# A float32 attention, expert and relu² kernel: the float64 weights converted earlier by way of DRAM, and half of the last network in seven block products

## The chip, the core and the metric

The kernel runs on one core of a Trainium2 chip. The core has a matrix engine (TensorE, PE in the profile), a vector engine (VectorE, DVE), a scalar engine (ScalarE, ACT), a general engine (GpSimd, POOL) and an engine whose queue issues most transfers (SyncE, SP); every queue works its instructions in order. The time is the device time of one launch in microseconds. Three runs of the kernel before took 679.74 to 681.3 us, median 680.23.

## The reference

Three parts follow on each other, all in float32 unless said otherwise: an attention with a window of 128, four dense experts whose sum is weighted per token, and a network with a squared relu.

```python
x = attention(q, k, v)                     # 2 x 8 heads, 576 positions, 64 wide -> 1152 x 512
p = domain_probs / (domain_probs.sum(-1, keepdims=True) + 1e-09)
for e in range(4):                         # w1: 512 x 1024, w2: 1024 x 512 each
    out += p[:, e:e + 1] * (np.maximum(x @ w1[e], 0.0) @ w2[e])
h = np.maximum(out @ w_in, 0.0)            # w_in: 512 x 2048, float64
y = (h * h @ w_out).astype(np.float32)     # w_out: 2048 x 512, float64
```

w_in and w_out arrive as float64 (their float32 draws are multiplied by a float64 scale); the kernel sees them as pairs of 32-bit integers.

## The kernel before

A float32 product is made of three matmuls on a rounded type (fp32r): with a = ah + al and b = bh + bl, the products ah·bh, al·bh and ah·bl are summed in PSUM. So each weight tile has a high part (wh, or ha and hs) and a low part (wl, la, ls), each activation too (xh, xl; hmem for the hidden layer). The last network is cut in two of the experts' size, so that there are six networks e = 0 to 5 with F = 1024: e = 4 and 5 are the first and the second half of w_in and w_out.

Tokens lie along the columns of the first GEMM and along the rows of the second. The first GEMM comes in items. A single item (`gemm1`) makes 128 hidden features for a chunk of 384 tokens with 12 matmuls. A pair item (`gemm1_pair`) makes 256 hidden features for all of 512 or 640 tokens as a 2 x 2 block product in seven block products for eight, each of 6 matmuls of 256 or 320 columns: 42 matmuls. It needs forms of the weights (sums of blocks, `w_forms`) and of the tokens (`x_forms`). Its epilogue reads the block products out of PSUM as p1 and p5 (copies by ScalarE, lines 989 and 994), adds them (VectorE, 975), applies relu (ScalarE, 979) and takes the low part (VectorE, 980). Three PSUM banks are reused inside an item: p1 must have been copied before the fourth block product writes that bank on, u2 before the fifth.

Expert 0 and the first half of expert 1 run in single items, the rest of the experts in 20 pair items, and both halves of the last network, e = 4 and 5, in 24 single items each. The second GEMM (`gemm2`, `gemm2_pair`, 512 columns a matmul) of an item is put off: items wait in the list `pend` and are flushed one or more items later (`flush_one`), so that the epilogue has time. e = 5 has 288 matmuls in its first GEMM and 216 in its second; its epilogue is relu on ScalarE (1037), the square on VectorE (1038), rounding on ScalarE (1039), low part on GpSimd (1040).

Up to the end of the first items a planner orders the work by costs and due times. From there the order is written by hand: the loop over `items` issues the matmuls, and after every few of them `fill(share, us)` moves a program clock on by `us` and takes some closures from a list of background work, the weights' preparation above all, whose number is set by `pace` so that a weight is ready some 14 us before its item. `loads` issues the next weight's transfer on SP when enough of the 24 weight buffers (4 KB per partition each) are free. Each weight item of e < 4 is one transfer of 512 KB, rounded to its high part by ScalarE and, for the low part, subtracted by GpSimd in pieces of 128x256.

A weight of e = 4 or 5 comes in two raw halves of 512 KB (128x512 float64 each) and goes through `split64` in its own buffers (wroom), just before its use: ScalarE scales the magnitude of the upper words (199), VectorE takes the sign (203), clamps (206), joins the low bits (210) and shifts and joins (214), all as integers; then ScalarE rounds the half to wh (349) and VectorE takes wl (429). This happens from about 418 us on.

Of the kernel before, what the change touches and what calls it, by code (L numbers as in the profile page):

```python
# [8 lines left out]
F32 = mybir.dt.float32  # L9
# [121 lines left out]
def kernel(  # L131
# [29 lines left out]
    ctx.enter_context(tc.manual_schedule())  # L161
    const = ctx.enter_context(tc.tile_pool(name="const", bufs=1))
# [21 lines left out]
    def split64(raw, n, t):  # L184

        lo, hi = raw[:, :, 0], raw[:, :, 1]  # L190
        stt = nc.vector.scalar_tensor_tensor

        def begin():
            if not room:
                room.extend(w_tile([P, 2, n], F32, "wroom")[0] for _ in range(3))
            room.append(room.pop(0))
            t["a"], t["b"] = room[-1][:, 0, :], room[-1][:, 1, :].bitcast(I32)
            t["ai"] = t["a"].bitcast(I32)
            nc.scalar.activation(out=t["a"], in_=hi.bitcast(F32), func=ACTF.Abs, scale=65536.0)

        return [
            begin,
            lambda: nc.vector.tensor_scalar(
                out=t["b"], in0=hi, scalar1=-(1 << 31), scalar2=None, op0=ALU.bitwise_and
            ),
            lambda: nc.vector.tensor_scalar(
                out=t["a"], in0=t["a"], scalar1=8053063680.0, scalar2=2.0,
                op0=ALU.min, op1=ALU.max,
            ),
            lambda: stt(  # L210
                out=t["b"], in0=lo, scalar=29, in1=t["b"],
                op0=ALU.logical_shift_right, op1=ALU.bitwise_or,
            ),
            lambda: stt(
                out=t["ai"], in0=t["ai"], scalar=3, in1=t["b"],
                op0=ALU.logical_shift_left, op1=ALU.bitwise_or,
            ),
        ]

# [10 lines left out]
    room = []  # L230
    raws = {}
    ready = set()
    carry = []
# [12 lines left out]
    def w_load(i):  # L246
        e, g, k = order[i]
        src, nk, nf = w_src(e, g, k)
        raws[i] = []
        if e < E:  # L250
            raw = w_tile([P, nk * nf], F32, "wraw")
            nc.sync.dma_start(out=raw[0].rearrange("p (k f) -> p k f", k=nk), in_=src)
            raws[i].append(raw)
        else:
            n = nk // 2
            for h in range(2):
                raw = w_tile([P, n * nf, 2], I32, "wraw64")
                nc.sync.dma_start(
                    out=raw[0].rearrange("p (k f) t -> p k (f t)", k=n).bitcast(mybir.dt.int64),
                    in_=src[:, h * n:(h + 1) * n, :],  # L260
                )
                raws[i].append(raw)


# [10 lines left out]
    def w_forms(i):  # L275
# [7 lines left out]
        def begin():  # L283
            for name, n in (("ha", 6), ("hs", 8), ("la", 6), ("ls", 8)):
                t[name] = w_tile([P, n, P], F32R, name)
            w1t[e, g] = [t[x] for x in ("ha", "hs", "la", "ls")]
# [25 lines left out]
        def done():  # L312
            for o in range(0, 8, 2):
# [14 lines left out]
            lambda: (part_lo(4, 2, a22), free.append(buf)),  # L328
# [4 lines left out]
    def w_ops(i):  # L333
# [3 lines left out]
        n = nk if e < E else nk // 2  # L337
        parts = (w1t, w2t)[k]
# [3 lines left out]
        def begin():  # L342
            parts[e, g] = [w_tile([P, nk, nf], F32R, name) for name in ("wh", "wl")]

        def part(full, h):
            (hi, _), (lo, _) = parts[e, g]
            ks = slice(h * n, (h + 1) * n)
            full = full.rearrange("p (k f) -> p k f", k=n)
            nc.scalar.activation(out=hi[:, ks, :], in_=full, func=ACTF.Copy)  # L349
            if e >= E:  # L350
# [1295 lines left out]
```

## Time and profile before

| | |
|---|---|
| median of three runs | 680.23 us |
| profiled execution | 680.41 us, its span 678.4 us |
| granted TensorE clock, mean over the span | 0.995 |
| busy, share of the span: PE, DVE, ACT, POOL | 98%, 60%, 44%, 42% |
| moved by DMA | 47.60 MB |

The profile shows one execution. Its span goes from the first to the last instruction that the trace holds; the time of the execution has 2.0 us more around it. The slices of the page show the stages: TensorE's digit is 8 in the first slice (17 us), 7 in the last and 9 in all between, and the granted clock is at full speed from the second slice on. The pair items lie between 227 and 457 us, the start of the last network's first half (e = 4) at about 475, its second half (e = 5) at about 575 to 674. A busy TensorE is not TensorE at its peak: to see what a matmul costs in a stream without holes, the distance from one start to the next is read, since the durations of neighbours overlap.

### The profile page before, as it was taken

What the parts mean: (1) busy time and instruction counts of PE and PEld (TensorE: products, weight loads), DVE (VectorE), ACT (ScalarE), POOL (GpSimd) and SP (SyncE); (2) the same over time, 40 slices, a digit from 0 to 9 for tenths busy, and PEclk for the clock granted to TensorE, in tenths of its full rate; (3) what the DMA queues carried; (4) which work ended last, traced back from release to release, by engine and by line L of the source; (5) the groups of instructions that cost most, each with busy time, mean ns of one, the idle gap of its engine ahead of it and who ended that gap; (6) DMA issues with size and microseconds to landing.
All of it is one profiled execution on the core that took longest, in us unless ns stands there. A gap on an engine that the chain in (4) does not pass through costs nothing.

```text
span 678.4 us, 10321 instructions
## 1 busy us (share of the span) xinstructions
PE 667.0 (98%) x3792; PEld 595.5 (88%) x3792; DVE 404.9 (60%) x905; ACT 297.2 (44%) x697; POOL 283.8 (42%) x359
## 2 busy tenths in 40 slices
PE   8999999999999999999999999999999999999997
PEld 7777888889999998888989899898899999999996
DVE  4798898854665346435553654887777788721212
ACT  5798787632331423133333324333555544422222
POOL 3799996518770455143464533000222222222222
PEclk7999999999999999999999999999999999999999
DMA  7933222021300112101201111136114200010101
GB/s 208 284 100 96 71 77 62 11 94 62 125 32 0 32 32 94 39 28 59 63 31 63 63 63 63 62 125 240 70 63 157 92 1 1 1 44 3 46 1 46
DMA packets 37106, 47.60 MB, mean 70 GB/s; under 512 B 3392, under 2 KB 25408, under 8 KB 37056
## 3 DMA queue, kind: packets, MB, share of 16 engines
q1 hardware_dynamic: 37056, 46.95, 22.1%
q8 instruction: 29, 0.48, 0.3%
q14 instruction: 21, 0.17, 0.1%
HBM read 44.58 MB, written 2.36 MB: 69 GB/s over the span
## 4 chain that ended last, share of the span: by engine, by line
PE 89%; POOL 4%; ACT 3%; DVE 2%; issue 1%; SPq 1%; DMA 1%; POOLq 0%; ACTq 0%
PE hps L865 24%; PE yacc L1051 23%; PE yacc L1019 18%; PE hps L965 15%; PE xps L660 3%; PE tp L788 2%; POOL wl L429 2%; PE sc L740 2%; POOL ts L776 1%; PE hps L1460 1%; SPq L1284 1%; DMA pt<-in_probs_dram 1%; POOL vl L429 1%; PE xtp L1084 0%; DVE st L768 0%
## 5 line engine op out<-in xcount | busy, mean ns | idle before, releaser
L1051 PE MATMUL yacc<-wh,hmem 128*128 128x512 f32 x488 | 157.1, 391 | 0.0
L1040 POOL TENSOR_TENSOR hmem<-r,hmem 128x384 fp32r<-128x384 f32 x48 | 50.0, 1042 | 200.7 <-ACT hmem L1039 198.9
L865 PE MATMUL hps<-xh,wh 128*128 128x384 f32 (+1 forms) x352 | 115.3, 328 | 1.0 <-DVE xl L1089 1.0
L1019 PE MATMUL yacc<-wh,hmem 128*128 128x512 f32 x360 | 115.3, 391 | 0.0
L865 PE MATMUL hps<-xh,wl 128*128 128x384 f32 (+1 forms) x352 | 113.8, 323 | 0.0
L865 PE MATMUL hps<-xl,wh 128*128 128x384 f32 (+1 forms) x352 | 113.6, 323 | 0.0
L1051 PEld LDWEIGHTS yacc<-wh,hmem 128*128 128x128 f32 x488 | 91.6, 188 | 18.6
L1051 PE MATMUL yacc<-wl,hmem 128*128 128x512 f32 x244 | 95.4, 391 | 0.0
L1019 PEld LDWEIGHTS yacc<-wh,hmem 128*128 128x128 f32 x360 | 67.6, 188 | 13.5
L429 POOL TENSOR_TENSOR wl<-wraw,wh 128x256 fp32r<-128x256 f32 (+1 forms) x70 | 61.9, 912 | 24.6 <-ACT wh L349 19.1
L1019 PE MATMUL yacc<-wl,hmem 128*128 128x512 f32 x180 | 70.3, 390 | 0.0
L865 PEld LDWEIGHTS hps<-xh,wh 128*128 128x128 f32 x352 | 66.3, 188 | 2.4 <-DVE xl L1089 1.2
L865 PEld LDWEIGHTS hps<-xl,wh 128*128 128x128 f32 x352 | 66.3, 188 | 0.9 <-issue 0.2
L865 PEld LDWEIGHTS hps<-xh,wl 128*128 128x128 f32 x352 | 66.3, 188 | 0.0
L1038 DVE TENSOR_TENSOR r<-hps,r 128x384 f32<-128x384 f32 x48 | 26.7, 556 | 64.2 <-ACT r L1037 64.2
L429 POOL TENSOR_TENSOR ls<-wsum,hs 128x256 fp32r<-128x256 f32 x40 | 32.3, 838 | 77.2 <-ACT hs L310 77.2
L1051 PEld LDWEIGHTS yacc<-wl,hmem 128*128 128x128 f32 x244 | 45.8, 188 | 8.6
L1037 ACT ACTIVATE r<-hps 128x384 f32<-128x384 f32 x48 | 23.4, 488 | 65.0 <-PE hps L865 65.0
L776 POOL TENSOR_SCALAR ts<-ts,st 128x256 f32<-128x256 f32 (+2 forms) x80 | 40.5, 521 | 25.7 <-DVE st L771 11.5
L979 ACT ACTIVATE hmem<-c 128x256 fp32r<-128x256 f32 (+1 forms) x60 | 25.8, 445 | 53.2 <-DVE c L975 52.4
L975 DVE TENSOR_TENSOR u<-hps,p 128x256 f32<-128x256 f32 (+1 forms) x40 | 18.2, 456 | 51.6 <-PE hps L965 50.2
L1069 DVE SCALAR_TENSOR_TENSOR y<-yacc,pt,y 128x512 f32<-128x512 f32 x54 | 38.9, 746 | 14.5 <-PE yacc L1019 8.2
(140 smaller groups left out, 1399.9 us busy)
## 6 DMA issues: line engine op xcount, KB each, us to landing
wraw<-in_w_dram SPq DMA_DIRECT2D x32, 512.0 KB, 3.6
wraw<-in_w_in_dram SPq DMA_DIRECT2D x16, 512.0 KB, 4.7
wraw<-in_w_out_dram SPq DMA_DIRECT2D x16, 512.0 KB, 3.4
rq<-in_qT_dram SPq DMA_DIRECT2D x8, 256.0 KB, 7.2
out_dram<-y SPq DMA_DIRECT2D x8, 256.0 KB, 2.1
rk<-in_kT_dram SPq DMA_DIRECT2D x8, 192.0 KB, 6.0
rv<-in_v_dram SPq DMA_DIRECT2D x8, 192.0 KB, 4.0
rq<-in_qT_dram SPq DMA_DIRECT2D x8, 192.0 KB, 2.6
```

The lines of the kernel that those rows point to most:

```text
L429: e.tensor_tensor(out=out, in0=in0, in1=f32(in1), op=ALU.subtract)
L660: nc.tensor.matmul(out=xps[:, :, o0:o0 + w], lhsT=l_, rhs=r_, start=(i == 0 and l_ is wh_ and r_ is hi), stop=(i == len(mm) - 1 and l_ is ...
L776: nc.gpsimd.tensor_scalar(out=ts[0:n, g, :], in0=ts[0:n, g, :], scalar1=st[0:n, 2, g:g + 1], scalar2=1.0, op0=ALU.mult, op1=ALU.mult,)
L865: nc.tensor.matmul(out=ps, lhsT=l_[:, k, cs], rhs=r_[:, k, cols], start=(k == 0 and r_ is xh and l_ is wh and not second), stop=(k == KT - ...
L965: nc.tensor.matmul(out=ps, lhsT=a[l_][:, k, :], rhs=b[r_][:, k, :], start=start and k == 0 and l_ == r_, stop=stop and k == 1 and l_ == 1, ...
L979: nc.scalar.activation(out=hh, in_=src, func=ACTF.Relu)
L1019: nc.tensor.matmul(out=y, lhsT=l_[:, ns], rhs=r_[:, fo, :], start=(first and fo == 0 and j == 0), stop=(last and fo == FTQ - 1 and j == 2),)
L1037: nc.scalar.activation(out=r, in_=ps, func=ACTF.Relu)
L1038: nc.vector.tensor_tensor(out=r, in0=ps, in1=r, op=ALU.mult)
L1040: nc.gpsimd.tensor_tensor(out=hl, in0=r, in1=f32(hh), op=ALU.subtract)
L1051: nc.tensor.matmul(out=y, lhsT=l_[:, ns], rhs=r_[:, fo, :], start=(first and j == 0), stop=(last and j == 2),)
L1069: nc.vector.scalar_tensor_tensor(out=yt, in0=y, scalar=pt[:, nt, e:e + 1], in1=yt, op0=ALU.mult, op1=ALU.add)
```

## The change

It has two parts.

The first: all 32 raw halves of w_in and w_out are converted during the experts. `convert` takes three weight buffers (two for raw halves, one for two results) as soon as three kept ones are free, which is during the first half of expert 1. Per half it issues one ScalarE and four VectorE instructions (266 to 277: magnitude, clamp, shift left by 3, join of the sign, join of the low bits); ScalarE's queue then stores the float32 half to DRAM (line 251, 256 KB) and loads the next raw half but one (239, 512 KB). These closures run at no more than 0.6 per us, at a single item's end, in a flush, or at the end of a pair item (`calm`). When a network weight's turn comes, `w_load` takes it from DRAM as float32 on SP in one transfer of 512 KB, and it is prepared like any expert's: ScalarE rounds, GpSimd subtracts in four pieces. `split64` and its buffers are gone.

The second: e = 5 runs in 8 pair items (4 weight groups x 2 token chunks), so its first GEMM has 336 matmuls, 168 of 256 and 168 of 320 columns; the second GEMM is the same. The epilogue of these items has the square (989 to 1009). The token forms for them are made by VectorE during e = 4. The weight forms (`w_forms`) take one buffer less.

On ScalarE at the end of the last 256-column item of expert 1: first the rows of before, where c_2884 to c_2886 are sums of an item's block products, p_2986 and p_2987 the next item's first copies.

```order
L979 ACTIVATE hmem<-c_2884 128x256 [waits DVE_49]
L979 ACTIVATE hmem<-c_2885 128x256 [waits DVE_49]
L979 ACTIVATE hmem<-c_2886 128x256 [waits DVE_49]
L989 ACTIVATE p_2986<-hps 128x320 [waits PE_49,Activation_49]
L994 ACTIVATE p_2987<-hps 128x320 [waits PE_49,Activation_49]
```

Now the same place, with p_3045 the next item's first copy; the numbers in brackets name what a row waits for, DMAHW a transfer.

```order
L1008 ACTIVATE hmem<-c_2937 128x256 [waits DVE_49]
L1008 ACTIVATE hmem<-c_2938 128x256 [waits DVE_49]
L266 ACTIVATE wconv<-wraw_2433 128x512 [waits DMAHW2_49,DMAHW1_49]
L251 DMA w_3007<-wconv 128x512
L239 DMA wraw_2432<-in_w_in_dram 128x2x256 [waits Activation_49]
L266 ACTIVATE wconv<-wraw_2432 128x512 [waits DMAHW6_49,DMAHW5_49]
L251 DMA w_3007<-wconv 128x512 [waits DVE_49]
L239 DMA wraw_2433<-in_w_in_dram 128x2x256 [waits DMAHW0_49,Activation_49]
L1018 ACTIVATE p_3045<-hps 128x320 [waits PE_49]
```

Between the last relu and p stand two halves, each with a store and a raw load; the second half reads wraw_2432, which the row above it loads.

At the end of the next 320-column pair of items in expert 1 the rows after the last relu are, in words: a half, store, load, the rounding of the weight sums hs, a half that reads what was just loaded, store, load, the rounding of a w2 weight, and then the next item's p. Before there were hs, p and the rounding behind p's.

On ScalarE at the start of e = 4: r and hmem are the epilogue of a single item, xh rounds a tile of transposed tokens for the same network, wh a weight. Before:

```order
L1037 ACTIVATE r<-hps 128x384 [waits PE_49]
L1039 ACTIVATE hmem<-r 128x384 [waits DVE_49]
L349 ACTIVATE wh<-wroom 128x512
L1088 ACTIVATE xh<-xtp 128x4x128 [waits PE_49]
L1037 ACTIVATE r<-hps 128x384 [waits PE_49]
L1039 ACTIVATE hmem<-r 128x384 [waits DVE_49]
```

And now:

```order
L1066 ACTIVATE r<-hps 128x384 [waits PE_49,Activation_49]
L1068 ACTIVATE hmem<-r 128x384 [waits DVE_49]
L266 ACTIVATE wconv<-wraw_2433 128x512 [waits DMAHW7_49,DMAHW0_49]
L251 DMA w_5321<-wconv 128x512
L239 DMA wraw_2432<-in_w_in_dram 128x2x256 [waits Activation_49]
L1118 ACTIVATE xh<-xtp 128x4x128 [waits PE_49]
```

The rounding of a weight half is gone, and a half, its store and a raw load stand ahead of xh. Some items later two halves in a row (half, store, load, a half that reads what was just loaded, store, load) come ahead of the copies of the second GEMM's results and the next xh, where two weight halves and their roundings stood among those copies.

On TensorE in e = 5: the end of a flush (yacc) and the start of the next item (hps), before:

```order
L1051 MATMUL yacc<-wh,hmem 128x512 x2
L1051 MATMUL yacc<-wl,hmem 128x512
L1051 MATMUL yacc<-wh,hmem 128x512
L865 MATMUL hps<-xh,wh 128x384 [waits DVE_49]
L865 MATMUL hps<-xl,wh 128x384
L865 MATMUL hps<-xh,wl 128x384
```

And now, where ht_5845 is a form of the tokens:

```order
L1048 MATMUL yacc<-wl,hmem 128x512
L1048 MATMUL yacc<-wh,hmem 128x512
L978 MATMUL hps<-xh,ha 128x320
L978 MATMUL hps<-xl,ha 128x320
L978 MATMUL hps<-xh,la 128x320
L978 MATMUL hps<-xh,ha 128x320
L978 MATMUL hps<-xl,ha 128x320
L978 MATMUL hps<-xh,la 128x320
L978 MATMUL hps<-ht_5845,hs 128x320 [waits DVE_49]
```

Instead of 12 matmuls of 384 columns on the plain weights there are groups of six of 320 (or 256) on weight forms.

The diff, cut to what the text speaks of:

```diff
     def w_load(i):
         e, g, k = order[i]
         src, nk, nf = w_src(e, g, k)
-        raws[i] = []
+        raw = w_tile([P, nk * nf], F32, "wraw")
         if e < E:
-            raw = w_tile([P, nk * nf], F32, "wraw")
             nc.sync.dma_start(out=raw[0].rearrange("p (k f) -> p k f", k=nk), in_=src)
-            raws[i].append(raw)
         else:
...
+            nc.sync.dma_start(out=raw[0], in_=single[i])
+        raws[i] = [raw]
+    single = {}
+    stored = set()
+    keep = [3]
...
+    def convert():
+        n = KT * FQ // 2
+        todo = [(i, h) for i in range(len(order)) if order[i][0] >= E for h in range(2)]
+        places = [w_tile([P, n, 2], I32, "wraw64") for _ in range(2)]
+        both, buf = w_tile([P, 2, n], F32, "wconv")
+        raw, ops = {}, []
+        at = {}
+        def load(j, eng):
+            i, h = todo[j]
+            src, nk, nf = w_src(*order[i])
+            raw[j] = places[j % 2][0]
+            m = nk // 2
+            eng.dma_start(
+                out=raw[j].rearrange("p (k f) t -> p k (f t)", k=m).bitcast(mybir.dt.int64),
+                in_=src[:, h * m:(h + 1) * m, :],
+            )
+            at["raw", j] = clock["now"] + 6.0
+        def swap(j):
+            i, h = todo[j]
+            if not by(at["out", j]):
+                return False
+            if h == 0:
+                single[i] = scratch.tile([P, 2 * n], F32, name=f"w{i}")
+            nc.scalar.dma_start(out=single[i][:, h * n:(h + 1) * n], in_=both[:, j % 2, :])
+            at["gone", j] = clock["now"] + 5.0
+            if h:
+                stored.add(i)
+            if j + 2 < len(todo):
+                load(j + 2, nc.scalar)
+        def steps(j):
+            a = both[:, j % 2, :]
+            ai = a.bitcast(I32)
+            def begin():
+                if not (by(at["raw", j]) and by(at.get(("gone", j - 2), 0.0))):
+                    return False
+                hi = raw[j][:, :, 1]
+                nc.scalar.activation(out=a, in_=hi.bitcast(F32), func=ACTF.Abs, scale=65536.0)
+            def shift():
+                nc.vector.tensor_scalar(
+                    out=a, in0=a, scalar1=8053063680.0, scalar2=2.0, op0=ALU.min, op1=ALU.max
+                )
+                nc.vector.tensor_scalar(
+                    out=ai, in0=ai, scalar1=3, scalar2=None, op0=ALU.logical_shift_left
+                )
+            def join(part, amount, op):
+                nc.vector.scalar_tensor_tensor(
+                    out=ai, in0=raw[j][:, :, part], scalar=amount, in1=ai, op0=op,
+                    op1=ALU.bitwise_or,
+                )
+                at["out", j] = clock["now"] + 2.5
+            ops = [
+                begin, shift, lambda: join(1, -(1 << 31), ALU.bitwise_and),
+                lambda: join(0, 29, ALU.logical_shift_right),
+            ]
+            if j:
+                ops.insert(1, lambda: swap(j - 1))
...
+            return ops
+        for j in range(len(todo)):
+            ops += steps(j)
+        for j in range(2):
+            load(j, nc.sync)
+        return ops
...
+            free.insert(0, buf)
+            t["ls"] = w_tile([P, 8, P], F32R, "ls")
+            w1t[e, g] = [t[x] for x in ("ha", "hs", "la", "ls")]
...
+        (raw, buf), = raws.pop(i)
+        def run():
+            held = (w1t, w2t)[k][e, g] = [w_tile([P, nk, nf], F32R, name) for name in ("wh", "wl")]
+            hi, lo = (x.rearrange("p k f -> p (k f)") for x, _ in held)
+            nc.scalar.activation(out=hi, in_=raw, func=ACTF.Copy)
             for o in range(0, nk * nf, 2 * P):
-                rest("POOL", *(x[:, o:o + 2 * P] for x in (lo_, full_, hi_)))
+                rest("POOL", *(x[:, o:o + 2 * P] for x in (lo, raw, hi)))
             spent("POOL", 3.0)
...
+            free.append(buf)
+            ready.add(i)
+        return [run]
...
-        def relu(i, j, src):
+        def relu(i, j, src, place=None):
             hh, hl = (x[:, j * n:(j + 1) * n] for x in h[i])
+            if e >= E:
+                r = src if place is None else place
+                if place is None:
+                    nc.vector.scalar_tensor_tensor(
+                        out=r, in0=src, scalar=0.0, in1=src, op0=ALU.max, op1=ALU.mult
+                    )
+                else:
+                    nc.scalar.activation(out=r, in_=src, func=ACTF.Relu)
+                    nc.vector.tensor_tensor(out=r, in0=src, in1=r, op=ALU.mult)
+                nc.scalar.activation(out=hh, in_=r, func=ACTF.Copy)
+                eng = nc.vector if i else nc.gpsimd
+                eng.tensor_tensor(out=hl, in0=r, in1=f32(hh), op=ALU.subtract)
+                if not i:
+                    spent("POOL", 0.9)
+                return
...
-        relu(0, 0, pa)
+        relu(0, 0, pa, c22)
...
+    items = [x + (False,) for x in items]
+    pairs = set()
+    for e in range(1, NE):
+        for r in range(0, NQ, 2):
+            if (e, r) == (1, 0) or e == E:
+                fs = range(r * FTQ, (r + 2) * FTQ)
+                items += [(e, ch, f, False) for ch in range(len(CHUNKS)) for f in fs]
+            else:
+                items += [(e, ch, g, True) for ch in range(len(PAIRS)) for g in (r, r + 1)]
+                pairs |= {(e, r), (e, r + 1)}
...
-        return 5 if (e, g) in pairs and k == 0 else 2 if e < E or room else 5
+        return 4 if (e, g) in pairs and k == 0 else 2
     def loads():
         while wnext["load"] < len(order):
             i = wnext["load"]
             wait = i - wnext["ops"]
-            wide = order[i][0] >= E
-            if wait >= 3 or len(free) < (2 if wide else 1) + takes(wnext["ops"]):
+            if wait >= 3 or len(free) < 1 + takes(wnext["ops"]) + keep[0]:
+                return
...
-    def fill(share, us):
+    def fill(share, us, calm=False):
         clock["now"] += us
         x_turn[0] += 1
-        if xbg and x_turn[0] % 2:
+        if xbg and (x_turn[0] % 2 or x_late):
             if xbg[0]() is not False:
                 xbg.pop(0)
-                if not xbg:
-                    free.extend(fxbuf)
+        conv_due[0] = min(conv_due[0] + RATE * us, 6.0)
+        for _ in range(3):
+            if conv and (calm or share == 1.0) and conv_due[0] >= 1.0 and conv[0]() is not False:
+                conv_due[0] -= 1.0
+                conv.pop(0)
...
+        if keep[0] and e and len(free) >= keep[0]:
+            keep[0] = 0
+            conv += convert()
...
+            if e == E and not x2todo and not x_late and (fxkeep or len(free) > 4):
+                fxbuf[:] = [x[1] for x in fxkeep]
+                fx_room()
+                x_late.append(1)
+                (x0_most, x0_last), (x1_most, x1_last) = x_forms(0, "DVE"), x_forms(1, "DVE")
+                xbg += x0_most + x1_most + x0_last + x1_last
+                xbg.append(lambda: free.extend(fxbuf))
+                x_rest = [len(x1_last) + 1]
...
-    tail = ys.pop((NE - 1, len(CHUNKS) - 1))
-    for tile_ in tail:
-        for e, ch, f, h, _ in pend:
-            gemm2(e, ch, f, h, [tile_], f == 0, f == FT - 1)
-        evac(NE - 1, len(CHUNKS) - 1, [tile_])
+    while pend:
+        flush_one()
```

## Rows read from the trace of the kernel before

**Rows 1.** Four stretches: start:end, length, busy by engine, PE clock, DMA share, GB/s.

```profile
227.00:457.00 230.00, 229.36 (x1350) 207.96 (x1350) 124.82 (x245) 75.66 (x159) 88.16 (x118) 1.00 0.18 60
420.00:457.00 37.00, 37.00 (x220) 33.78 (x219) 30.07 (x63) 12.75 (x28) 0.00 (x0) 1.00 0.33 111
475.00:575.00 100.00, 99.00 (x508) 89.99 (x508) 77.26 (x141) 54.78 (x106) 25.71 (x24) 1.00 0.19 65
575.00:674.00 99.00, 99.00 (x504) 90.38 (x504) 30.89 (x54) 27.53 (x55) 24.29 (x24) 1.00 0.05 19
```

**Rows 2.** What PE waited for, 227 to 674: sum us, times, longest.

```profile
PE hps L865 <- DVE xl L1089: 1.0, 1, 1.0
PE hps L965 <- DVE u L975: 0.4, 1, 0.4
```

**Rows 3.** The chain that ended last, in e=5: start us, us, what.

```profile
575.21 8.34 PE hps L865 x48
...
657.94 8.34 PE hps L865 x48
666.29 7.75 PE yacc L1051 x34
```

**Rows 4.** Timeline of PE, edges of pair items: start us, us, instruction.

```profile
403.44 0.30 PE L965 MATMUL hps<-xh,ha 128*128 128x320 f32 x1
...
409.61 0.39 PE L1019 MATMUL yacc<-wh,hmem 128*128 128x512 f32 x1
...
416.44 0.28 PE L965 MATMUL hps<-xh,ha 128*128 128x256 f32 x1
...
421.55 0.40 PE L1019 MATMUL yacc<-wh,hmem 128*128 128x512 f32 x1
```

**Rows 5.** Timeline of DVE and POOL, end of two pair items.

```profile
400.24 1.91 DVE L980 SCALAR_TENSOR_TENSOR hmem<-c,hmem 128x320 fp32r<-128x320 f32 x2
...
411.38 0.90 DVE L980 SCALAR_TENSOR_TENSOR hmem<-c,hmem 128x320 fp32r<-128x320 f32 x2
...
400.81 0.99 POOL L292 TENSOR_TENSOR wsum<-wraw,wsum 128x256 f32<-128x256 f32 x1
```

**Rows 6.** Instructions by form: line, shapes, count, busy us, mean ns, idle before.

```profile
L199 ACT ACTIVATE wroom<-wraw 128x512 f32<-128x512 f32 x32 | 21.1, 660 | 0.0
...
L210 DVE SCALAR_TENSOR_TENSOR wroom<-wraw,wroom 128x512 int32<-128x512 int32 x32 | 21.9, 684 | 0.0
L214 DVE SCALAR_TENSOR_TENSOR wroom<-wroom 128x512 int32<-128x512 int32 x32 | 21.8, 680 | 0.0
...
L206 DVE TENSOR_SCALAR wroom<-wroom 128x512 f32<-128x512 f32 x32 | 14.7, 458 | 1.8 <-ACT wroom L199 1.8
L203 DVE TENSOR_SCALAR wroom<-wraw 128x512 int32<-128x512 int32 x32 | 13.4, 419 | 0.0
...
L429 POOL TENSOR_TENSOR wl<-wraw,wh 128x256 fp32r<-128x256 f32 x56 | 43.3, 804 | 24.4 <-ACT wh L349 19.1 <-issue 5.0
```

**Rows 7.** DMA issues of line 258, 380 to 420: ns of an issue, landing.

```profile
L258 SPq DMA_DIRECT2D wraw<-in_w_in_dram x4: 368/373/421, 380.5 to 418.9; - x4
...
DMA to landing us min/median/max: 3.2/3.4/5.0
```

**Rows 8.** Timeline of ACT around one pair item.

```profile
404.58 0.44 ACT L989 ACTIVATE p<-hps 128x320 f32<-128x320 f32 x1 [2.99 <-PE hps L965]
...
410.88 0.87 ACT L979 ACTIVATE hmem<-c 128x320 fp32r<-128x320 f32 x2 [0.96 <-DVE c L975]
411.65 1.04 ACT L310 ACTIVATE hs<-wsum 128x1024 fp32r<-128x1024 f32 x1
```

**Rows 9.** Timeline of ACT, DVE and PE at the network's start.

```profile
476.64 0.58 ACT L1088 ACTIVATE xh<-xtp 128x512 fp32r<-128x512 f32 x1
...
492.80 0.61 ACT L1088 ACTIVATE xh<-xtp 128x512 fp32r<-128x512 f32 x1
...
478.50 0.44 PE L865 MATMUL hps<-xh,wh 128*128 128x384 f32 x1 [1.00 <-DVE xl L1089]
```

More of the change, by code (lines that the diff above doesn't have):

```diff
@@ L951, in x_forms @@
         )
+    WIDE = max(n for _, n in CHUNKS)
     def gemm1_pair(e, ch, g):
@@ L1035, in gemm1 @@
         else:
-            r = late["f"].tile([P, n], F32, tag="r", name="r", bufs=2)
+            r = late["f"].tile([P, WIDE], F32, tag=("p1", "p5")[f % 2], name="r")[:, 0:n]
             nc.scalar.activation(out=r, in_=ps, func=ACTF.Relu)
@@ L1195, in loads @@
             wait = i - wnext["ops"]
-            wide = order[i][0] >= E
-            if wait >= 3 or len(free) < (2 if wide else 1) + takes(wnext["ops"]):
+            if wait >= 3 or len(free) < 1 + takes(wnext["ops"]) + keep[0]:
+                return
+            if order[i][0] >= E and i not in stored:
                 return
@@ L1206, in bg_some @@
                 i = wnext["ops"]
-                if i == wnext["load"] or len(free) < takes(i):
-                    if carry and i == len(order):
-                        carry.pop(0)()
+                if i == wnext["load"] or len(free) < takes(i) + keep[0]:
                     return False
@@ L1546, with fx_room @@
     attn_close()
-    fxwork, fxbuf = zip(*(w_tile([P, 2 * PAIRS[1][1]], F32, "fxwork") for _ in range(2)))
+    fxwork, fxbuf, fxkeep, x_late, conv = [], [], [], [], []
+    conv_due, RATE = [0.0], 0.6
+    def fx_room():
+        free[:0] = fxbuf
+        fxwork[:], fxbuf[:] = zip(*(w_tile([P, 2 * PAIRS[1][1]], F32, "fxwork") for _ in range(2)))
+    fx_room()
     x_free = [0]
@@ L1557, in want @@
             bg_run()
-            while carry:
-                carry.pop(0)()
             if i not in ready:
                 loads()
+                while wnext["load"] == wnext["ops"] and conv:
+                    assert conv.pop(0)() is not False
+                    loads()
                 assert len(free) >= takes(wnext["ops"]) and wnext["ops"] < wnext["load"]
@@ L1575 @@
         if two:
-            assert ch < len(PAIRS) - 1 or not xbg
+            while xbg and (ch or e > E and len(xbg) > x_rest[0]):
+                clock["force"] = True
+                assert xbg.pop(0)() is not False
+                clock["force"] = False
             h = gemm1_pair(e, ch, f)
@@ L1591 @@
         loads()
-        if (e, f) == (1, FT // 2 - 1) and not two:
+        if (e, f) in ((1, FT // 2 - 1), (E, FT - 1)) and not two:
             x_free[0] = CHUNKS[ch][0] + CHUNKS[ch][1]
@@ L1599 @@
             fill(1.0, 2.1)
-        last = (e, ch, f) in ((NE - 1, len(CHUNKS) - 1, FT - 1), (1, len(CHUNKS) - 1, FT // 2 - 1))
+        last = not two and (e, ch, f) in ((1, len(CHUNKS) - 1, FT // 2 - 1), (E, len(CHUNKS) - 1, FT - 1))
         left = LAG if last else (1, len(pend), len(pend), 0)[f % 4] if not two else 1
```

114 lines of the change are left out of this document (16 added, 98 removed).

## The prediction

> **What bounds the kernel now.** I read the busy time by stretch first, with the granted clock beside it: from 227 to 674 us TensorE is at the upper of its two levels (granted clock 1.00, 2.4 GHz) and busy 229.36 of 230, 99.00 of 100 and 99.00 of 99 us [rows 1]. Then what TensorE waited for in that stretch: two waits, 1.0 and 0.4 us in sum over 447 us [rows 2]. So the second two thirds of the kernel are a stream of matmuls without holes: an edit gains there only by issuing fewer or shorter matmuls, and loses whatever hole it opens. The chain that ended last shows the stream's composition in the last network: six times 48 matmuls of the first GEMM in 8.34 us, between them the second GEMM, at the end 34 matmuls in 7.75 us [rows 3].
>
> Everything up to the single items of expert 1 keeps its instructions and their order, so I take its time as it is.
>
> **What leaves TensorE.** The second half of the last network (e=5) has its first GEMM in 288 matmuls of 384 columns; by the chain that is 6 x 8.34 = 50.04 us [rows 3]. The pair form does it in 8 items of 42 matmuls, four with 256 columns and four with 320. The kernel already runs such items in its experts, so their price is in the trace, as the distance from an item's first matmul to the first matmul of the second GEMM behind it: 421.55 - 416.44 = 5.11 us for 256 columns and 409.61 - 403.44 = 6.17 us for 320 [rows 4]. Together 4 x 5.11 + 4 x 6.17 = 45.12 us. The second GEMM keeps its 216 matmuls of 512 columns. Gain: 50.04 - 45.12 = **4.92 us**, provided that the pair items run as gapless here as there.
>
> Does the longer epilogue of e=5 fit? In the experts the pair's last result leaves VectorE at 411.38 + 0.90 = 412.28, that is 2.67 us after the last matmul of the item ended at about 409.61 [rows 4, 5]. Squaring adds to each of the two last results one more VectorE pass of 0.64 us at most and a rounding of 0.44 us on ScalarE (half of 0.87) [rows 8]: 2.67 + 2 x (0.64 + 0.44) = 4.8 us. TensorE meanwhile has the previous item's second GEMM, 24 matmuls at 7.75/34 = 0.228 us, 5.47 us, or 30, 6.83 us (416.44 - 409.61) [rows 3, 4]. It is hidden by 0.6 us or more; at nothing. If that cover is gone it costs 8 times the excess.
>
> **What the conversion removes and adds.** Gone are the conversions in 128x512 halves just before use; they lay beside a stream that did not wait [rows 2], so removing them gains nothing by itself. Added: the same 32 halves earlier, through the experts, each with 0.66 us on ScalarE (L199's form) and on VectorE 0.419 + 0.458 + 0.684 + 0.680 = 2.24 us [rows 6], and three DMA issues: the store and the next raw load on ScalarE's queue at 0.37 us of the engine each, the later float32 load on SP [rows 7]. About 20 of the halves fall into the stretch of pair items: VectorE goes from 124.82 to at most 124.82 + 20 x 2.24 = 170 of 230 us, a share of 0.74. Between 420 and 457 us it already stands at 30.07 of 37, 0.81, with no wait of TensorE [rows 1, 2]. ScalarE goes from 75.66 to about 75.66 + 20 x (0.66 + 0.74) = 104 of 230. Shares alone thus forbid nothing; what counts is where a queued instruction waits. GpSimd gets the low parts of the network weights, 16 x 4 x 0.804 = 51 us [rows 6], over some 200 us in which it is busy 25.71 + 24.29 [rows 1]; hidden. The DMA share was 0.18 and 0.19 [rows 1]; storing and reloading 8.4 MB each way does not fill it.
>
> In a normal pair item ScalarE does one half at the end, and its next raw load has a whole item (10.6 to 13 us) to land against 3.2 to 5.0 us [rows 7]: nothing. The order shows three places where the wait for a raw load stands one row behind the issue of that load, on an engine whose next job is TensorE's.
>
> **Place A, end of the last 256-column item of expert 1.** Let T be the end of the item's first GEMM. ScalarE's last relu ends at 411.75, T + 2.14 [rows 8]. Behind it: first half 0.66, store and load issue 0.74 (T + 3.5), the load lands 3.2 to 5.0 after its issue at T + 3.2 (T + 6.4 to 8.2), second half 0.66, two issues 0.74, and only then the next item's p1 (0.44 [rows 8]): T + 8.2 to 10.0. TensorE needs p1's PSUM bank at its fourth block, after 5.47 us of second GEMM and 18 x 6.17/42 = 2.64 us: T + 8.1. Queued behind p1 are u2 on VectorE and the rest of the item, so the wait passes straight through. Hole 0.1 to 1.9; near the median landing of 3.4 it is 0.3, near the upper 1.9: I take **0.8**.
>
> **Place B, the last 320-column item there.** As A, with a 1.05 us rounding of the sums and one of a weight in the chain: p1 at T + 9.2 to 11.0; needed at T + 6.83 + 18 x 5.11/42 = T + 9.0. Hole 0.2 to 2.0, w_out's loads being the quicker: **0.6**.
>
> **Place C, start of the network (e=4).** TensorE's one wait of 1.00 us there, at 478.50, ends with xl, the low part of a transposed token tile; ScalarE rounded the tile at 476.64 [rows 9]. Now a half and two issues stand ahead of that rounding (0.66 + 0.74 = 1.4 us) where another 128x512 rounding, about L199's 0.66, stood: between 0.2 (part of the issues hidden) and 0.8 more, **0.6**. Some 14 us on, two halves and a wait for a load just issued stand ahead of the xh of 492.80 [rows 9]: 0 to 1.3, **0.5**.
>
> **VectorE beside GpSimd.** The same pair of relu remainders took 1.91 us at 400.24 and 0.90 at 411.38 [rows 5]; GpSimd was at work on weight sums beside the first. Conversion moves from a stretch where GpSimd has 0.00 of 37 us to one where it has 88.16 of 230 [rows 1]. Per item it can cost nothing (slack after p1 is 0.8 us and more) or one such second; over three items at most 2.5 us, at least 0; I take **0.25**, near the trace's own record of 0.4 us waited for u2 [rows 2].
>
> The page "SBUF — State Buffer" of the Trainium skill, section "Who interferes with whom", says that a VectorE instruction with two SBUF inputs and a GpSimd instruction that reads SBUF exclude one another, whichever is later blocking until the other ends. By that rule the two joining steps of every half are hit, not a few, and VectorE's 2.24 us would be nearer 3; the pair in rows 5 agrees in direction, but no run here shows the conversion itself beside GpSimd. By the rule the time is that of the slower rival below, 685.5, which is worked out without it.
>
> **The sum**, in the profiled execution: 680.41 us (span 678.4 and 2.0 around it, 0.18 above the median of the runs, 680.23): 680.41 - 4.92 + 0.8 + 0.6 + 0.6 + 0.5 + 0.25 = **678.2 us**.
>
> **Rivals.**
> - *All covers hold.* Loads land at 3.2 us and the holes at A to C close: 680.41 - 4.92 = 675.5, and 674.8 if the 1.0 us wait at the network's start shrinks as well. For it: no wait of more than 1.0 us in 447 us. Against it: the orders at A and B put a wait for a DMA in ScalarE's queue, which before never held one so close behind its issue.
> - *Gain eaten.* A to C at their upper ends: 1.9 + 2.0 + 0.8 + 1.3 = 6.0 less 4.92, 681.5; at three quarters of them 680.0. For it: w_in's loads have a landing up to 5.0 [rows 7].
> - *Slower: conversion in the way in every pair item.* The mechanism is VectorE's joining steps, blocked by GpSimd as the 1.91 us pair was, so that u2 (or ScalarE's p1, held behind a store that waits for the join) comes late for the fifth block. The place is each of the 20 pair items; with 0.5 us each it is 10 - 4.92 and up, 685.5 at least. It decides from (4.92 + 1.4)/20 = 0.32 us an item. Against it: VectorE at 0.81 without a wait [rows 1, 2]; for it: there GpSimd was idle.
> - *The change does not do what it says*: a weight not stored in time would make TensorE wait for it. The order has the last half stored in the first third of e=4, one network ahead of its use; I give it nothing of its own.
>
> **How the numbers follow.** This kernel's measurement tells 0.2%, 1.4 us, from no change. Forecast (677 to 679.5) 0.45, of which 0.32 faster; all covers hold 0.25; eaten 0.17; slower 0.13. So faster 0.32 + 0.25 = 0.57, same 0.13 + 0.17 = 0.30, slower 0.13. The range goes from the lowest case, 674.8, to 682.0, past the eaten one; a tenth above it, little below.
>
> **What would show it.** Right: pair items in e=5 at 5.11 and 6.17 us; a wait of TensorE for the first GEMM's bank released by ScalarE's p1, once at the end of each half of expert 1; a wait at the xl of the network's start of 1.2 to 2 us; VectorE at 0.70 to 0.74 of the pair stretch. Wrong: waits of some tenths in most pair items (slower), waits for hmem or wh in e=5 (epilogue or weights late), or no waits at all (675.5).

## The result: slower by 1.3%

The changed kernel takes 689.12 us (median of 4 runs, 688.5 to 690.23) against 680.16 for the kernel before beside it: ratio 1.0131, 95% interval 1.0111 to 1.0151. Forecast was 678.2. The profiled execution took 688.5 us with a span of 686.7.

What TensorE waited for from 150 us on (total, times, longest), after:

```profile
PE yacc L1080 <- POOL hmem L1069: 4.7, 3, 3.0
PE hps L978 <- DVE u L989: 3.8, 4, 1.7
PE hps L978 <- ACT p L1018: 1.6, 2, 1.1
PE hps L876 <- DVE xl L1119: 1.3, 1, 1.3
```

Before there were two lines, 1.0 and 0.4 us [rows 2]; now 11.4 us, and the largest is for GpSimd, of which the prediction expected no wait. The stages, by the starts of their first matmuls: the pair items of the experts went from 245.2 to 251.7 us, +5.3 in the first six (the holes lie in the second to the fifth) and +1.3 in the last three items; e=4 from 102.8 to 103.0, though 27 matmuls of its second GEMM (6.1 us) now fall behind its end, so it lost 6.3; e=5 from 99.1 to 100.2 with those 6.1 us in it, so it gained 5.0. The last is the forecast gain; the chain in e=5 shows it (start, us, what):

```profile
582.16 5.11 PE hps L978 x42
587.27 6.15 PE yacc L1080 x27
593.42 5.12 PE hps L978 x42
598.54 5.47 PE yacc L1048 x24
604.01 6.15 PE hps L978 x42
```

The four stretches (columns as in [rows 1]), pair items, the two parts of e=4, the rest:

```profile
227.00:479.00 252.00, 246.16 (x1425) 220.88 (x1425) 185.18 (x320) 96.61 (x187) 129.73 (x160) 1.00 0.36 119
479.00:520.00 41.00, 39.74 (x213) 36.38 (x212) 21.12 (x35) 17.90 (x34) 9.26 (x9) 1.00 0.28 94
520.00:565.00 45.00, 40.14 (x202) 35.46 (x201) 32.22 (x36) 20.37 (x37) 41.83 (x40) 1.00 0.12 36
565.00:682.00 117.00, 117.00 (x665) 105.77 (x664) 64.42 (x121) 35.89 (x77) 43.44 (x52) 1.00 0.08 27
```

The granted clock is 1.00 in all of them, so nothing of this execution's loss is the clock's. GpSimd stands idle for three quarters of e=4's first 41 us (9.26) and is full in the next 45 (41.83). What it does there (start, us, instruction; in brackets the idle time before it and what ended it):

```profile
530.96 3.49 POOL L440 TENSOR_TENSOR la<-wraw,ha 128x256 fp32r<-128x256 f32 x3
534.52 4.78 POOL L440 TENSOR_TENSOR ls<-wsum,hs 128x256 fp32r<-128x256 f32 x4
539.27 3.37 POOL L440 TENSOR_TENSOR wl<-wraw,wh 128x256 fp32r<-128x256 f32 x4
542.72 0.72 POOL L326 TENSOR_TENSOR wsum<-wraw 128x256 f32<-128x256 f32 x1
543.40 0.99 POOL L1069 TENSOR_TENSOR hmem<-r,hmem 128x384 fp32r<-128x384 f32 x1
...
544.45 0.73 PE L1080 MATMUL yacc<-wh,hmem 128*128 128x512 f32 x2 [3.03 <-POOL hmem L1069]
```

e=5's weight forms stand in GpSimd's queue ahead of e=4's own low part, hmem. The four ls pieces take 4.78 us here, beside VectorE's token forms; in the experts' pair items of the same trace four of them take 2.80 to 3.67.

In the first pair items there are two kinds of hole. ScalarE at place A:

```profile
248.40 0.65 ACT L266 ACTIVATE wconv<-wraw 128x512 f32<-128x512 f32 x1
248.53 1.31 ACTq L239 DMA_DIRECT2D wraw<-in_w_in_dram  x1
254.02 0.66 ACT L266 ACTIVATE wconv<-wraw 128x512 f32<-128x512 f32 x1 [4.97 <-DMA wraw<-in_w_in_dram]
254.04 0.33 ACTq L251 DMA_DIRECT2D w<-wconv  x1
254.47 0.39 ACTq L239 DMA_DIRECT2D wraw<-in_w_in_dram  x1
254.91 0.44 ACT L1018 ACTIVATE p<-hps 128x320 f32<-128x320 f32 x1 [0.23 <-ACT wconv L266]
```

The load issued at 248.5, which landed 5.4 us later, is awaited 4.97 us with p1 behind it. And VectorE in the second item:

```profile
236.04 1.22 DVE L277 SCALAR_TENSOR_TENSOR wconv<-wraw,wconv 128x512 int32<-128x512 int32 x1
237.19 0.96 DVE L269 TENSOR_SCALAR wconv<-wconv 128x512 f32<-128x512 f32 x1
238.19 0.85 DVE L272 TENSOR_SCALAR wconv<-wconv 128x512 int32<-128x512 int32 x1
239.07 2.26 DVE L277 SCALAR_TENSOR_TENSOR wconv<-wraw,wconv 128x512 int32<-128x512 int32 x2
241.25 2.05 DVE L1098 SCALAR_TENSOR_TENSOR y<-yacc,pt,y 128x512 f32<-128x512 f32 x3
243.23 0.40 DVE L989 TENSOR_TENSOR u<-hps,p 128x256 f32<-128x256 f32 x1
```

Seven microseconds of conversion and results without a gap, and u, for which TensorE waits, behind them. GpSimd works on weight forms all the while. The five conversion steps take 5.25 us here; where GpSimd is idle, steps of the same lines take 0.69, 0.42 and 0.43 us in this trace, an estimate of 2.9 for the five.

### The profile page after: what moved, and what is told of

The parts are those of the page before. It is cut to its first block, busy times and chain, and to the rows that moved or that the text cites. A ratio compares the mean times of both kernels' runs of the same rounds, so it can differ in the third digit from the quotient of the medians.

```text
span 686.7 us, 10703 instructions
## 1 busy us (share of the span) xinstructions
PE 664.3 (97%) x3840; PEld 590.0 (86%) x3840; DVE 470.0 (68%) x974; ACT 305.3 (44%) x705; POOL 360.5 (52%) x443
## 4 chain that ended last, share of the span: by engine, by line
PE 77%; POOL 7%; DVE 6%; ACT 3%; issue 2%; DMA 2%; SPq 1%; ACTq 0%; POOLq 0%
PE yacc L1048 22%; PE hps L978 20%; PE hps L876 14%; PE yacc L1080 13%; PE xps L671 3%; PE tp L799 2%; POOL wl L440 2%; PE sc L751 1%; POOL ls L440 1%; POOL ts L787 1%; POOL wsum L326 1%; DVE hmem L1009 1%; POOL la L440 1%; POOL hmem L1069 1%; PE hps L1485 1%
## 5 line engine op out<-in xcount | busy, mean ns | idle before, releaser
L440 POOL TENSOR_TENSOR wl<-wraw,wh 128x256 fp32r<-128x256 f32 (+1 forms) x118 | 101.8, 891 | 38.3 <-ACT wh L382 26.5
L876 PE MATMUL hps<-xh,wh 128*128 128x384 f32 (+1 forms) x256 | 83.2, 325 | 1.3 <-DVE xl L1119 1.3
L876 PE MATMUL hps<-xh,wl 128*128 128x384 f32 (+1 forms) x256 | 81.6, 319 | 0.0
L876 PE MATMUL hps<-xl,wh 128*128 128x384 f32 (+1 forms) x256 | 81.5, 318 | 0.0
L277 DVE SCALAR_TENSOR_TENSOR wconv<-wraw,wconv 128x512 int32<-128x512 int32 x64 | 51.0, 797 | 1.5
L1069 POOL TENSOR_TENSOR hmem<-r,hmem 128x384 fp32r<-128x384 f32 x24 | 26.9, 1121 | 47.8 <-ACT hmem L1068 47.7
L876 PEld LDWEIGHTS hps<-xh,wh 128*128 128x128 f32 x256 | 48.2, 188 | 2.5 <-DVE xl L1119 1.5
L326 POOL TENSOR_TENSOR wsum<-wraw 128x256 f32<-128x256 f32 x28 | 25.0, 893 | 47.8 <-PE hps L876 35.9
L876 PEld LDWEIGHTS hps<-xh,wl 128*128 128x128 f32 x256 | 48.2, 188 | 0.0
L1009 DVE SCALAR_TENSOR_TENSOR hmem<-c,hmem 128x256 fp32r<-128x256 f32 (+1 forms) x60 | 37.6, 650 | 11.6 <-ACT hmem L1008 10.7
```

Of the source, the lines that this page charges most:

```text
L277: nc.vector.scalar_tensor_tensor(out=ai, in0=raw[j][:, :, part], scalar=amount, in1=ai, op0=op, op1=ALU.bitwise_or,)
L326: nc.gpsimd.tensor_tensor(out=t["s"][:, o:o + 2, :], in0=x(), in1=y(), op=op)
L440: e.tensor_tensor(out=out, in0=in0, in1=f32(in1), op=ALU.subtract)
L876: nc.tensor.matmul(out=ps, lhsT=l_[:, k, cs], rhs=r_[:, k, cols], start=(k == 0 and r_ is xh and l_ is wh and not second), stop=(k == KT - ...
L1009: nc.vector.scalar_tensor_tensor(out=hl, in0=src, scalar=0.0, in1=f32(hh), op0=ALU.max, op1=ALU.subtract)
L1069: nc.gpsimd.tensor_tensor(out=hl, in0=r, in1=f32(hh), op=ALU.subtract)
```

## The experiments

Times are medians; "before" was 679.9 to 680.1 in all of them.

**e=4's low parts on VectorE from feature 4 on.**

```diff
-            nc.gpsimd.tensor_tensor(out=hl, in0=r, in1=f32(hh), op=ALU.subtract)
-            spent("POOL", 1.05)
+            eng = nc.gpsimd if f < FT // 2 else nc.vector
+            eng.tensor_tensor(out=hl, in0=r, in1=f32(hh), op=ALU.subtract)
+            if f < FT // 2:
+                spent("POOL", 1.05)
```

> The low parts of the squared hidden layer in the second half of e=4 (features 4 to 7 of each chunk) go to VectorE in place of GpSimd. Theory: the changed kernel's largest hole (TensorE waits 4.7 us in three places, the longest 3.0, for GpSimd's low part of e=4's hidden layer, 541 to 563 us) is a queue: GpSimd has e=5's weight forms and w2 low parts in front of that low part. Then these waits go, nothing comes in their place, and the time falls by 4.7 to 6 us, from 688.6 to 683 to 684. Rival: GpSimd is simply short of time in that stretch; then the weight forms are late for e=5 as well and the time stays within 1.5 us of 688.6, with a wait at e=5's start. Second rival: VectorE, busy there with the token forms, is late in GpSimd's place; 686 to 688, waits released by VectorE.

691.05 us. GpSimd's wait is gone, and a wait of the same size stands in its place, for VectorE's square:

```profile
PE hps L876 <- DVE r L1067: 3.7, 1, 3.7
```

e=4 took 103.5 us against 103.0, so the second rival is right in its mechanism, though not in its 686 to 688: both engines are short of time in that stretch. The rest of the longer time lies ahead of the edit, in pair items whose order is the same (254.8 us for 251.7 in the profiled executions): place A's load landed after 6.4 us, its hole was 2.3 us for 1.3, and the clock fell behind it (granted clock 0.72 as a mean of 256 to 262 us).

**A raw load counted as landed after 12 us**, `clock["now"] + 12.0` for `+ 6.0`.

> The program clock counts a raw load as landed 12 us after its issue, not 6, so that ScalarE's next half is ordered later. Theory: two holes of the first pair items (1.3 us at 254 and 0.7 + 0.8 us at 281 to 283) are ScalarE standing at the wait for a raw load that it has just issued, with p1 behind; then both go, 688.6 - 2.7 = 685.9. Rival: the half moves to a later item that has its own collision on VectorE, and the holes move rather than go: 687.5 to 689.

696.48 us, a miss by its own side effect: three halves in four pair items where there had been one in each, the conversion not done by e=5, forced there with 12.5 us of waits for ScalarE; and since its buffers never came free, the token forms of e=5 are left out. Only the stretch ahead is readable: the pair items took 246.2 us, 5.5 less than in the changed kernel.

**Without VectorE's part of the conversion.**

```diff
-                begin, shift, lambda: join(1, -(1 << 31), ALU.bitwise_and),
-                lambda: join(0, 29, ALU.logical_shift_right),
+                begin, lambda: None, lambda: None,
+                lambda: at.update({("out", j): clock["now"] + 2.5}),
```

> The four VectorE instructions of each conversion are left out (the stored weights are what ScalarE wrote); the loads, ScalarE's part and the stores stay. Theory of separate holes: the two waits for u in the first pair items (1.8 us at 242, 1.3 us at 268) and the three small ones at 438 to 462 (1.2 us) go, while ScalarE's load waits (2.7 us) and GpSimd's late low parts in e=4 (5.5 us) stay: 688.6 - 4.6 = 684, at most 1.5 lower if the earlier stores pull the loads forward. Rival, VectorE's conversion work is behind everything: nearly all holes go, 676 to 678. Rival, the extra transfers on ScalarE's queue are behind it: little changes, 687 to 689.

682.67 us. The pair items took 246.7 us, ScalarE's load waits shrank to one of 1.1, and GpSimd's longest wait in e=4 stayed at 3.0. So VectorE's steps are behind most of the pair items' loss, not behind e=4's largest hole. The smaller waits for hmem behind that hole went, but the clock fell there instead (last section), so e=4 still took 102.4 us.

**Without the conversion** (`w_src(e - E, g, k)` loaded in place of `single[i]`, no buffers kept).

> The conversion is left out altogether: the two network halves load the float32 weights of experts 0 and 1 in place of w_in and w_out, so what is timed is the second part of the change alone (e=5 in pair items, weights by ScalarE and GpSimd). Theory: e=5 gains its 4.9 us in full, the pair items of the experts run as before, and the hole in e=4 stays, since e=5's forms make it and not the conversion: 680.2 - 4.9 + 5.5 = 681 (680 to 682). Rival, the hole in e=4 comes from the conversion's lateness or its buffers (the forms start late because conversion holds buffers until 512 us): it shrinks, 675.3 to 677.5.

674.58 us, no wait over 0.6. But the token forms fell away here as well, so it does not say which of the two made e=4's hole. Hence the next run but three.

**A raw load counted as landed after 8 us.**

> The program clock counts a raw load as landed 8 us after its issue, not 6: too long for a second half within one flush (5.5 to 6.9 us), short enough for one half in every pair item. All else as in the changed kernel. Theory: the holes of the first four pair items (6.1 us in sum, of which before had 1.6) come from items that take two halves: ScalarE stands at a load just issued, and VectorE's steps pile up ahead of u. Then they shrink to what before had, 688.6 - 4.5 to 5.5 = 683 to 684; the hole in e=4 stays. Rival: the holes come from the conversion beside GpSimd's weight forms there, however many halves an item takes; then most of them stay, 687 to 689.

682.71 us, 6.4 less: ratio to before 1.0039 (1.0024 to 1.0054). Of the holes in the second to the fifth item only that in the second is left (2.2 us).

**One load held back.**

```diff
+            if i == 8 * E + 9 and wnext["ops"] < i:
+                return
```

> One load is held back: the second GEMM's weight of e=5's first group is loaded only after that group's weight forms have been begun; all else as in the changed kernel. Theory: the forms need four free buffers, and from the start of e=4 until the conversion ends (some 40 us) there are three, the conversion holding three of its own; GpSimd is idle then and short of time afterwards, when forms, e=4's low parts and VectorE's token forms fall together. With one load less the forms begin some 40 us earlier and the hole in e=4 (5.5 us in all) goes for the most part: 682.5 to 684.5. Rival: the collision of GpSimd and VectorE over the token forms alone makes the hole; it stays above 4 us, 687 to 689.

686.18 us, 2.9 less, half of the expected. e=5's first forms start at 490 us, not 525. But the weight held back now has its four low pieces ahead of hmem, beside VectorE's token forms, for 4.16 us, and one hole of 2.8 us is left:

```profile
526.50 4.16 POOL L440 TENSOR_TENSOR wl<-wraw,wh 128x256 fp32r<-128x256 f32 x4 [3.05 <-ACT hmem L1068]
...
532.11 0.73 PE L1080 MATMUL yacc<-wh,hmem 128*128 128x512 f32 x2 [2.77 <-POOL hmem L1069]
```

Behind it the clock fell for some microseconds (last section).

**Both.**

> The two edits together (8 us for a raw load, and the load held back). Theory of two independent causes: both savings add, 688.6 - 10 to 11 = 677.5 to 679, faster than the kernel before by 0.2 to 0.4%. Rival: with the conversion ending one item later the token forms start later and collide with GpSimd in the second half of e=4 all the same: 680 to 683.

679.31 us, ratio 0.9993 (0.9984 to 1.0002); 9.8 less than the changed kernel, where 6.4 and 2.9 had gone singly: they add. The token forms begin at 532 us here, after the pieces that stood in their way in the run before. In e=4 GpSimd now works more evenly and waits for it are down to 0.3 us:

```profile
479.00:520.00 41.00, 39.53 (x208) 36.02 (x207) 21.80 (x35) 19.55 (x37) 19.90 (x22) 1.00 0.30 103
520.00:565.00 45.00, 44.69 (x224) 40.05 (x223) 32.75 (x43) 18.99 (x35) 29.33 (x29) 1.00 0.19 71
```

**The second part with all its work, without the conversion** (as above, but two buffers kept for the token forms).

> The conversion is left out (the network halves load the float32 weights of experts 0 and 1), and unlike the earlier run without it the token forms of e=5 are made by VectorE in e=4, in two buffers that are held from expert 1 on. This is the second part of the change with all its work. Theory: without the conversion's third buffer the weight forms begin early and nothing collides: e=5 gains 4.9 us and nothing is lost, 674.5 to 676. Rival: the token forms alone slow GpSimd so that e=4's hole comes back, 679 to 681.

675.36 us, ratio 0.9930 (0.9915 to 0.9945). The token forms run from 498 us on, and the same two stretches show no collision:

```profile
479.00:520.00 41.00, 40.44 (x211) 36.76 (x211) 19.69 (x29) 21.00 (x39) 20.98 (x25) 1.00 0.04 14
520.00:565.00 45.00, 45.00 (x231) 41.10 (x230) 21.29 (x28) 16.38 (x31) 23.04 (x26) 1.00 0.14 47
```

The second part gains 4.7 us; the conversion, with all that it sets off, costs 689.1 - 675.4 = 13.8. The last three pair items have their small holes here as well (1.1 us), so those are not the conversion's.

**Both, stores and raw loads on SP's queue** (`nc.sync` for `nc.scalar`).

> The kernel with both edits (8 us for a raw load, one load held back), and the conversion's stores and raw loads issued on SP's queue in place of ScalarE's. Theory: of the hole that is left in the second pair item (0.9 us at p1, 1.4 us at u, about 240 us), the first part is ScalarE standing some 4 us behind a store that waits for VectorE's join; it goes, and the two issues before xh at e=4's start go as well: 679.3 - 0.9 to 1.6 = 677.7 to 678.4. Rival: VectorE's steps alone make it, and ScalarE's place in the queue does not matter: 679 to 679.6. Second rival: weight loads on SP come late behind the waiting stores: over 680.

682.65 us, 3.3 more. The hole in the second item stays 2.2 us, so ScalarE's stand behind the store was no cause of its own; and SP, waiting for VectorE's joins, brings a weight late, as the second rival had it:

```profile
531.36 0.74 POOL L326 TENSOR_TENSOR wsum<-wraw 128x256 f32<-128x256 f32 x1 [6.47 <-DMA wraw<-w]
```

**Both, plain weights rounded in halves**, as two steps; hs is the slice of one half.

```diff
-            nc.scalar.activation(out=hi, in_=raw, func=ACTF.Copy)
+            nc.scalar.activation(out=hi[:, hs], in_=raw[:, hs], func=ACTF.Copy)
```

> The kernel with both edits, and each plain weight rounded by ScalarE in two halves of 128x512 as two steps (about 0.62 us each) in place of one of 128x1024 (1.05 us). Theory: the three small holes in the last pair items of expert 3 (0.8, 0.3, 0.3 us) come from a 1.05 us rounding between ScalarE's p5 and the relu of the fourth block product; they go: 679.3 - 1 to 1.5 = 677.8 to 678.3. Rival: VectorE's conversion steps make them; 679 to 679.6. Doubling the steps also moves the weights' preparation about, which may cost up to 1 us elsewhere.

678.85 us, ratio 0.9978 (0.9969 to 0.9988), at most half of the expected gain. The three small holes of the last pair items are gone from the trace (1.4 us); at e=4's start two waits for xl, 1.4 and 0.4, became one of 1.8. In the profiled execution most of the gain went elsewhere: behind the second item's hole the clock fell (granted clock 0.72 as a mean of 243 to 249 us), which it did not in that of the kernel with both edits, and the pair items took 247.5 us for 247.7. In the kernel with both edits the 1.05 us rounding stood between p5 and the relu whose bank TensorE wants:

```profile
431.14 0.39 ACT L1023 ACTIVATE p<-hps 128x256 f32<-128x256 f32 x1 [1.34 <-PE hps L978]
431.42 1.05 ACT L382 ACTIVATE wh<-wraw 128x1024 fp32r<-128x1024 f32 x1
432.37 0.37 ACT L1008 ACTIVATE hmem<-hps 128x256 fp32r<-128x256 f32 x1
```

**All of these together.**

> Both edits, SP's queue and the halved roundings together. If the last two theories hold, their savings add: 679.3 - 2 to 3 = 676.3 to 677.3, within 2 us of the second part of the change alone (675.4). If not, 678.5 to 679.6.

680.65 us: beside the halves alone (678.85) SP's queue costs 1.8 us here, where it cost 3.3; the theory's sum is missed.

**No conversion step in the first pair item** (on the kernel with halved roundings; raw loads at 6 us again in e=4).

```diff
+        if held[0]:
+            calm = False
...
+        held[0] = (e, ch, f, two) in ((1, 0, 2, True), )
```

> The kernel with both edits and the halved roundings, and no step of the conversion during the first pair item (end and flush); during e=4 a raw load is counted as landed after 6 us again, so that the conversion ends little later. Theory: the hole of 2.2 us in the second pair item is VectorE's conversion steps beside GpSimd's weight sums, which there follow on each other without a gap; with no step in that place it goes, 678.85 - 2 = 676.5 to 677.2, less up to 0.7 given back where the token forms now start later in e=4. Rival: GpSimd's backlog there delays the weight forms themselves, so the hole stays: 678.5 to 679.5.

676.09 us, ratio 0.9942 (0.9928 to 0.9955): faster than both kernels, 0.7 us above the second part alone. The holes in the experts' pair items are gone; the waits for u and p that are left lie in e=5:

```profile
PE hps L881 <- DVE xl L1124: 1.7, 1, 1.7
PE hps L983 <- DVE u L994: 0.6, 2, 0.4
PE hps L983 <- ACT p L1023: 0.5, 1, 0.5
```

The token forms begin at 531.8 us (498.2 in the second part alone) and end at 571.6, where e=5's first p and u stand behind them.

## Why the prediction was wrong

*What bounds the kernel*: right. TensorE's stream had no holes, and every hole that opened was paid in full.

*The gain of 4.92 us*: right. The pair items of e=5 run at 5.11 and 6.15 us, the longer epilogue is hidden (no wait of TensorE in e=5), and the second part alone measures 4.7.

*Places A, B, C*: right in mechanism, with A and B dearer than was taken. A cost 1.3 us (0.8 taken, up to 1.9), with a landing of 5.4 us. In the first run and with one load held back, whose orders are the same up to there, the landing was 6.4 and 5.9 and A cost 2.3 and 1.8: the 5.0 us that bounded the landing came from six loads [rows 7]. B cost 0.7 at p1 and 0.8 at u, which stood behind VectorE's steps for the half just loaded (0.6 taken, up to 2.0). C's first part cost 0.3 more than before and its second nothing.

*VectorE beside GpSimd at 0.25 us*: the term that was mis-sized. It cost 3.4 us in the second and fourth pair items, 2.7 more than before had there; 2.5 was the upper bound. The argument ran on shares (0.81 without a wait), and a share over 230 us says nothing of seven microseconds in a row: there weight forms on GpSimd, a half and a pile of results met in one item. The slower rival named this mechanism, but set it in each of 20 items; the items from 297 to 428 us lost nothing. What decides is where steps stack up, which the 8 us run, with one half an item, and the last run, with none in that one place, show. At 438 to 462 us another 1.2 us came from ScalarE's long roundings, which the prediction had counted nowhere.

*GpSimd's 51 us "hidden"*: the step that failed. GpSimd's added work was set against 200 us in which it was busy 50, without asking when a buffer lets it start. The amount was right: 94.5 us busy from 479 to 682 us, where 51 + 50 = 101 were counted. e=5's forms need four free buffers; with three held by the conversion there were three, until the conversion ended at about 520 us. Then forms, low parts and token forms fell into 45 us, each slower for the others. The 5.5 us of waits in e=4 are that. The runs show the buffers' part (one load held back, alone and with the other edit: forms earlier, 2.9 and 3.4 us less) and the part of the collision (the first run: moving work between the two engines moves the wait); the second part alone, with the token forms at 498 us, has neither.

Of the price of a half on VectorE, 2.24 us was the undisturbed one. The means after are higher (line, shapes, count, busy us, mean ns):

```profile
L277 DVE SCALAR_TENSOR_TENSOR wconv<-wraw,wconv 128x512 int32<-128x512 int32 x64 | 51.0, 797 | 1.5
L269 DVE TENSOR_SCALAR wconv<-wconv 128x512 f32<-128x512 f32 x32 | 20.3, 636 | 6.9 <-ACT wconv L266 6.8
L272 DVE TENSOR_SCALAR wconv<-wconv 128x512 int32<-128x512 int32 x32 | 18.4, 576 | 1.1
```

2 x 0.80 + 0.64 + 0.58 = 2.81 us. The mean of a join hides two prices: the 37 of 64 with GpSimd idle took 0.68 to 0.69 us, and 15 of the 18 with GpSimd at work throughout 1.11 to 1.22. The Trainium skill, page "SBUF — State Buffer", section "Who interferes with whom", says that both kinds of instruction can contend with GpSimd, the two-input one by its second read and tensor_scalar by its two-port modes; the trace agrees, with these 1.11 to 1.22 for 0.69 us and, for tensor_scalar, mostly 0.84 to 0.98 for 0.43 where GpSimd worked throughout. The prediction weighed the rule for the joins and let it go for the shares.

What stays open: the 0.7 us between the last kernel and the second part alone. By their profiled executions the last kernel loses 1.8 us in e=5, where p and u wait behind token forms that started 34 us later, and 1.1 at e=4's xl (1.8 for 0.7); it gains 1.7 in the pair items, above all by the halved roundings. Neither loss was tried.

## What to carry to other kernels

Work is hidden only if the buffers let it start where the engine is idle: for each added step, ask what must be free before it, and who holds that. Before pricing an engine by its share, look for the few microseconds in which its queue has several kinds of work in a row ahead of what the bounding engine waits for. A program clock that places a transfer's reader must allow for when the queue really gets to the issue, and not for the landing alone: 6 us, more than place A's landing of 5.4, put a wait of 4.97 us into ScalarE's queue, 8 us did not, and 12 us kept the conversion from ending in time.

## What the runs showed of the hardware

A hole of TensorE can cost more than its length. After the 2.8 us hole of the held-back load and after the 3.7 us one of the first run the granted clock fell to 0.57 and 0.72 as a mean of the next stretch, that is to the lower of its two levels (1.2 GHz) for part of it; the distance between 512-column matmuls was 0.43 us there, for 0.228. With the load held back (columns as in [rows 1]):

```profile
533.00:537.00 4.00, 4.00 (x12) 3.15 (x11) 2.17 (x2) 0.99 (x2) 2.68 (x3) 0.57 0.08 31
```

And with e=4's low parts on VectorE:

```profile
564.00:570.00 6.00, 6.00 (x23) 5.29 (x22) 4.19 (x9) 2.85 (x6) 0.00 (x0) 0.72 0.50 175
```

The same followed the 3.0 us hole of the run without VectorE's part (granted clock 0.57 as a mean of 538 to 546 us) and, with the halved roundings, the two holes of 2.2 us together in the second pair item (0.72 from 243 to 249 us). But the profiled execution of the changed kernel had a hole of 3.0 us without this, and the kernel with both edits the same 2.2 us without it, so the length of a hole alone does not decide. The other executions of the changed kernel had a mean clock of 0.987 to 0.989, against its 0.995, and took up to 1.7 us longer. That would fit such falls; their traces are not there to show it.

Moving issues off a compute engine's queue made things worse: on SP the stores' waits for VectorE delayed the weight loads behind them (6.47 us of GpSimd's idle time), and the kernel lost 3.3 us. And moving a subtraction from GpSimd to VectorE in a stretch where both are busy bought nothing: TensorE's waits there were 4.7 us for the one and 3.7 + 0.4 for the other, and e=4 took 103.0 and 103.5 us.
